# V in one transfer a pair instead of four, and GpSimd casting it across partition halves, later in its order

## The chip, the core and the metric

The kernel runs on one core of a Trainium2 chip. The core has five instruction streams that run side by side and meet through semaphores: PE (TensorE, matrix products), DVE (VectorE), ACT (ScalarE), POOL (GpSimd) and SP (SyncE, which only issues transfers). All transfers, whoever issues them, run on the core's 16 DMA engines. Two memories lie on the core: SBUF, with 128 partitions, and PSUM, where PE writes its products. The metric is the device time of one execution in microseconds (us). Three runs of the kernel before took 281.47, 281.88 and 282.79 us; the median is 281.88 us.

## The reference

An attention with a soft cap on the scores is followed by a soft mixture of experts whose tokens are the attention's outputs. The shapes are 8 batches, 12 heads, 448 tokens and 64 numbers a head, so 96 heads in all; then 3584 tokens of 768 numbers, 8 experts with 4 slots each, and a hidden width of 1024.

```python
scores = cap * tanh(q @ k.T / sqrt(64) / cap)          # cap = 30
attn   = softmax(scores)                               # over the keys
x      = (attn @ v)  -> (3584, 768)
logits = x @ phi                                       # (3584, 32)
d      = softmax(logits, over the tokens)
slots  = d.T @ x                                       # 32 slots
out_e  = relu(slots_e @ w1_e) @ w2_e                   # each expert, 4 slots
c      = softmax(logits, over the slots)
out    = c @ all the slots' outputs                    # (3584, 768), float32
```

Each token is a key and a value for the 448 tokens of its head. All inputs come as float32 from HBM.

## The kernel before, in words

**Pairs and quads.** Two heads make a pair (48 of them, numbered 0 to 47) and two pairs a quad (24). One pair's V is 2 x 448 x 64 float32 numbers, 224 KB. A head's 448 tokens are laid as 64 partitions of 7 tokens each: partition p of a half holds tokens 7p to 7p+6, and the 7 are called units here.

**The attention.** Q and K of a quad come by GpSimd's transfers, which also cast them to bf16 (`load`, line 290), are turned by PE (`transp`, L401, tiles `qps`, `kps`) and copied by DVE (`turned`, L410, L413). PE computes scores (`qk_chunk`, L444, tile `sc`, two buffers). ACT applies tanh to a chunk of them (`tanh_chunk`, L454) and the exponential to about two thirds of the chunks (`exp_part`, L458). For the other third DVE computes the exponential by a polynomial in eight steps (`poly_exp`, L478 to L486), with two scratch tiles, `xf` and `xp`. PE multiplies the result by V (`pv_mms`, L507), DVE normalises it (`norm_rec`, `norm_mul`, L515, L519), PE and DVE turn it (tile `xT`), and the logits and slot sums are gathered as it goes.

**V.** V of a pair lands in one of three buffers of `vraw` as float32, 128 partitions by 448 numbers. GpSimd casts it to bf16 into `vbd` (two buffers, one for each of two quads), which PE uses. In `vbd` each group of keys takes one unit from either head: the two heads' halves are arranged so that a matmul over 128 partitions sees both heads, with unit 3 of each head in a place of its own, whose other half is zero. For this the units of a head must lie partly in the upper partitions and partly in the lower. Before the change the transfers do that: `load_v` (L301 to L312) issues four of them, each 64 partitions by 4 or 3 units (1024 or 768 bytes a row). `vcast` (L417 to L423) is then one cast of 128 partitions by 6 units (L419) and two casts of 64 partitions by 1 unit (L423), all of which stay in their partitions.

**What sets the order.** Each engine runs its instructions in the order in which they were written. A string `PROGRAM` lists the steps, and `do` carries them out one by one: Q and T are scores and tanh, E an exponential on ACT, p a step of the polynomial, K and J the turning of K and Q, k and j its copies, A, t, B, u the four parts of a pair's product with V, r and m its normalisation, X, y, x the turning of the result, M one transfer of weights by GpSimd. At step u of pair n, `vcast_after(n)` writes the cast for pair n+4, which takes the place in `vbd` that pair n has just done with. A cast also issues the transfer of V three pairs on (SP). The steps K and J also issue the K and Q transfers two quads on, in GpSimd's order. So GpSimd's queue holds casts, K and Q transfers and weight transfers, each behind the one before.

**The weights.** GpSimd moves both weight matrices from HBM during the attention and casts them to bf16: w1 into SBUF (`w1b`), a part of w2 into SBUF (`w2u`), the rest back into HBM (`w2d`), 8 whole parts of 768 KB and 10 half parts of 384 KB. When the attention's buffers come free, SP reloads them (`reload`, L172 for whole and L174 for half parts, tiles `w2t`, two of them `raws`). The reloads are issued in one fixed order: half part 8, part 0, half parts 10 and 11, parts 1, 2, 3, half part 9, parts 4 to 7, half parts 12 to 17. Each waits for what lay at its place: half part 11 lies where `vraw` was, parts 1 and 2 take the places of `xf` and `xp`, half part 9 takes the place that the last two pairs' V had.

**The end.** After the last pair the two expert layers run (L882, L911), and the outputs go out by SP (L928) while DVE and ACT scale the tiles (L942, L944, L994, L996).

Of the kernel before, what the change touches and what calls it, by code (L numbers as in the profile page):

```python
# [18 lines left out]
P = 128  # L19
HP = 64  # L20
NT = 7
DH = 64
S = 448
CH = 6
CS = 3
# [5 lines left out]
W = DH + 1  # L31
# [7 lines left out]
def kernel(  # L39
# [224 lines left out]
    def part(x, off, *dims):  # L264
        return bass.AP(tensor=x.tensor, offset=x.offset + off, ap=[x.ap[0]] + [list(d) for d in dims])
# [8 lines left out]
    def quad_ap(nm, Q, h=None):  # L274
        b, hq = divmod(Q, NQB)
        off = (b * H + 4 * hq) * S * DH
        if h is not None:
            return bass.AP(tensor=srcs[nm].tensor, offset=off + 2 * h * S * DH,
                           ap=[[NT * DH, P], [1, NT * DH]])
        return bass.AP(tensor=srcs[nm].tensor, offset=off,  # L280
                       ap=[[NT * DH, P], [2 * S * DH, 2], [1, NT * DH]])
# [14 lines left out]
    def v_raw(Q, h):  # L296

        return raw_tile("kq"[h], (Q + 1) % 2).bitcast(F32) if Q == NQ - 1 else \
            vraw[:, (2 * Q + h) % NV, :]

    def load_v(Q, h):  # L301

        if Q < NQ:
            src = quad_ap("v", Q)
            long, short = slice(0, (CS + 1) * DH), slice((CS + 1) * DH, S)
            for r0, n, cols, at in ((0, 0, long, 0), (0, 1, short, CS + 1),
                                    (HP, 0, slice(0, CS * DH), CS + 1),
                                    (HP, 1, slice(CS * DH, S), 0)):
                sp.dma_start(out=v_raw(Q, h)[r0:r0 + HP, cols],
                             in_=bass.AP(tensor=src.tensor,  # L310
                                         offset=src.offset + (2 * h + n) * S * DH + at * DH,
                                         ap=[[NT * DH, HP], [1, cols.stop - cols.start]]))  # L312

    def init_vbd(n):
        t = vbds[n]
# [100 lines left out]

    def vcast(Q, h):  # L417
        raw, t = v_raw(Q, h), vbds[Q % 2]
        pool.tensor_copy(part(t[:, h, :, :], 0, [(CS + 2) * W, 2], [W, CS], [1, DH]),  # L419
                         part(raw, 0, [(CS + 1) * DH, 2], [DH, CS], [1, DH]))  # L420
        for n in range(2):
            r = slice(n * HP, n * HP + HP)
            pool.tensor_copy(t[r, h, CS + n, 0:DH], raw[r, CS * DH:(CS + 1) * DH])  # L423
        if 2 * Q + h + NV < NPAIR - 2:
            load_v(*divmod(2 * Q + h + NV, 2))

    def vcast_after(pr):

        Q, h = divmod(pr, 2)
        if Q + 2 < NQ:  # L430
            vcast(Q + 2, h)
# [252 lines left out]
    def spare(n, k=1):  # L684

        junk = home(k, [P, 4, P], F32, "junk")
        for _ in range(n):
            pe.matmul(junk, ones, wide(4), start=True, stop=True)

    def do(x, a, n):  # L690

        if x == "X":
            held["x", a] = home(n, [P, 2, S], BF16, "xps")
            x_mms(a, (0, 1, 2), held["x", a])
        elif x == "y":
            x_mms(a, (NF,), held["x", a])
        elif x == "t":
            pv_tail(a, 0, CA)
        elif x == "u":
            pv_tail(a, CA, NT)  # L700
            vcast_after(a)
        elif x == "x":
            x_copy(a, (0, 1) if a < NQ - 1 else (0,), held.pop(("x", a)))
        elif x == "e":
            es[a] = consts.tile([P, NG, NS], BF16, name="E", tag="E", bufs=3)
            act.activation(es[a], lps.pop(a), ACT.Exp)
        elif x == "R":
            held["R", a] = home(n, [P, 512], BF16, "eps")
            et_mms(a, held["R", a])
        elif x == "c":  # L710
            et_copy(a, held.pop(("R", a)))
        elif x == "W":
            held["W", a] = home(n, [P, NT], F32, "wps")
            ws_mms(a, held["W", a])
        elif x == "w":
            dve.reciprocal(winv[:, a, :], held.pop(("W", a)))
        elif x == "r":
            norm_rec(a, NT, pvs[a])
        elif x == "m":
            norm_mul(a, 0, NT, pvs.pop(a))  # L720
        elif x == "G":
            for i in range(a):
                pe.matmul(scores[n][:, i % CS, S:512], ones, ones[:, 0:512 - S], start=False,
                          stop=True, skip_group_check=True)
        elif x == "M":
            wjobs[a][0](*wjobs[a][1:])
        elif x == "O":
            reload_raw(a)
        elif x == "N":
            spare(a, n)  # L730
        elif x in "KJ":
            transp("kq"["KJ".index(x)], a, n)
        elif x in "kj":
            turned("kq"["kj".index(x)], a)
        else:
            {"Q": qk_chunk, "T": tanh_chunk, "E": exp_chunk, "p": poly_exp, "A": pv_first,
             "B": pv_rest, "L": logits, "S": slot_sums, "s": slot_add, "V": vcast,
             "F": fill}[x](*((a,) if n is None else (a, n)))
# [22 lines left out]

    for x, n in jobs:
        do(x, n[0], n[1] if len(n) > 1 else None)

    gl = NCH - 1
    last = NPAIR - 1
# [269 lines left out]
```

## Time and profile before

The profiled execution took 282.57 us on its own clock, of which the span, first to last instruction, is 280.7 us. All times below are counted from the start of that span.

| engine | busy, us | share of the span | instructions |
|---|---|---|---|
| ACT | 244.6 | 87% | 192 |
| DVE | 241.7 | 86% | 363 |
| PE | 234.1 | 83% | 4065 |
| POOL | 158.3 | 56% | 251 |

ACT and DVE are busy 9 tenths or more in every slice from about 14 us to about 225 us. That is the attention. After it come some 50 us in which no engine but the DMA is full. The page's line of DMA slices reads 9 (90% or more) nearly throughout. "Share of DMA" in a table of windows can exceed 1, since packets of two queues overlap on an engine.

In a timeline row the first number is the start, the second the time taken, then engine, line, operation, tiles written and read, shape, count, and in brackets how long the engine sat idle before and what released it. SPq means an issue in SP's queue.

### The profile page before, as it was taken

To read this page: it belongs to the slowest core of one execution; us is meant where nothing else is said; L and a number is where in the kernel's file an instruction comes from. 1 tells how busy PE (TensorE), PEld (TensorE's weight loads), DVE (VectorE), ACT (ScalarE), POOL (GpSimd) and SP (SyncE) were. 2 spreads that over 40 slices of the span, in tenths; PEclk is the share of its full clock that TensorE was granted. 3 is DMA by queue.
4 is the path that set the end of the run, shared out by engine and by line. 5 is a ranking of instruction groups with operands and counts; after the bars stand their busy time and mean duration, and the time that the engine had idled before them with its cause. 6 is when DMAs were issued, how large, how long until landed. Compare 5 with 4: busy or idle time off the path is not lost.

```text
span 280.7 us, 9632 instructions
## 1 busy us (share of the span) xinstructions
PE 234.1 (83%) x4065; PEld 149.4 (53%) x4065; DVE 241.7 (86%) x363; ACT 244.6 (87%) x192; POOL 158.3 (56%) x251
## 2 busy tenths in 40 slices
PE   8899879987898988888889989888889999798520
PEld 6435555564464756555656655655656675433200
DVE  3799999999999999999999999999999983258540
ACT  4999999999999999999999999999999992247420
POOL 8489567266877499858754969979342132000000
PEclk9999999999999999999999999999999999999955
DMA  6999999999999999999999999999999989989995
GB/s 177 224 168 221 222 222 206 222 212 221 224 231 191 216 214 227 222 228 224 226 225 226 222 229 224 217 223 218 219 229 243 277 329 403 398 308 366 407 413 243
DMA packets 51788, 69.56 MB, mean 248 GB/s; under 512 B 5921, under 2 KB 38305, under 8 KB 51745
## 3 DMA queue, kind: packets, MB, share of 16 engines
q0 software_dynamic: 27840, 35.77, 73.1%
q1 hardware_dynamic: 23616, 32.95, 35.9%
q8 instruction: 32, 0.52, 0.7%
q10 hardware_dynamic: 288, 0.23, 0.3%
q14 instruction: 12, 0.09, 0.1%
HBM read 93.68 MB, written 21.23 MB: 409 GB/s over the span
## 4 chain that ended last, share of the span: by engine, by line
ACT 68%; DVE 11%; DMA 9%; PE 5%; issue 2%; DVEq 0%; SPq 0%; ACTq 0%
ACT ex L454 30%; ACT ex L458 19%; ACT exg L454 9%; ACT exg L458 7%; DMA w2t<-w2d_None 4%; DMA out_dram<-ob 3%; PE so_ps L911 2%; DMA out_dram<-obh 1%; PE sc L444 1%; DMA raws<-in_q_dram 1%; DVE xp L484 1%; DVE xp L482 1%; DVE ex L485 1%; DVE xq L519 1%; DVE xp L481 1%
## 5 line engine op out<-in xcount | busy, mean ns | idle before, releaser
L454 ACT ACTIVATE ex<-sc 128x1344 f16<-128x1344 f32 (+1 forms) x87 | 108.9, 1372 | 1.3 <-PE sc L444 1.3
L444 PE MATMUL sc<-qT,kT 64*128 64x448 bf16 x384 | 67.8, 353 | 8.4 <-ACT ex L454 5.0
L458 ACT ACTIVATE ex<-ex 128x2688 bf16<-128x2688 f16 x27 | 68.4, 2546 | 0.0
L419 POOL CAST vbd<-vraw 128x384 bf16<-128x384 f32 x46 | 36.2, 787 | 43.1 <-DMA vraw<-in_v_dram 19.1
L507 PE MATMUL pv<-vbd,ex 128*128 128x65 bf16 (+2 forms) x1041 | 54.9, 200 | 5.7 <-DVE xT L576 1.4
L507 PEld LDWEIGHTS <-ex 128*128 128x128 bf16 (+1 forms) x1070 | 42.4, 101 | 21.1 <-issue 6.1
L423 POOL CAST vbd<-vraw 64x64 bf16<-64x64 f32 x92 | 51.9, 565 | 2.8
L454 ACT ACTIVATE exg<-sc 128x1344 f16<-128x1344 f32 x26 | 33.6, 1372 | 0.0
L444 PEld LDWEIGHTS <-kT 64*128 64x128 bf16 x384 | 18.7, 93 | 24.9 <-issue 11.4
L519 DVE TENSOR_TENSOR xq<-pv,rec 128x448 bf16<-128x448 f32 x47 | 28.5, 613 | 0.4
L458 ACT ACTIVATE exg<-exg 128x2688 bf16<-128x2688 f16 x11 | 27.7, 2520 | 0.0
L484 DVE TENSOR_TENSOR xp<-xp,xf 128x2688 f16<-128x2688 f16 x17 | 26.5, 1560 | 0.0
L482 DVE TENSOR_TENSOR xp<-xp,xf 128x2688 f16<-128x2688 f16 x17 | 26.4, 1556 | 0.0
L401 PEld LDWEIGHTS <-raws 128*64 128x64 bf16 x616 | 19.6, 109 | 11.2 <-issue 9.8
L290 POOL DMA_DIRECT2D raws<-in_q_dram x22 | 17.2, 782 | 11.9 <-PE qps L401 9.5
L485 DVE TENSOR_TENSOR ex<-ex,xp 128x2688 uint16<-128x2688 uint16 x15 | 23.1, 1539 | 0.0
L507 PE MATMUL pv<-vbd,exg 128*128 128x65 bf16 (+2 forms) x322 | 20.5, 199 | 2.9 <-DVE xq L519 1.9
L290 POOL DMA_DIRECT2D raws<-in_k_dram x22 | 17.0, 774 | 9.1 <-PE kps L401 5.0
L507 PEld LDWEIGHTS <-exg 128*128 128x128 bf16 (+1 forms) x322 | 14.3, 101 | 7.5 <-issue 4.1
L401 PE MATMUL kps<-ident,raws 128*64 128x128 bf16 x308 | 12.7, 221 | 3.4 <-DVE qT L413 0.9
L483 DVE TENSOR_SCALAR xp<-xp 128x2688 f16<-128x2688 f16 x17 | 15.0, 885 | 0.0
L481 DVE TENSOR_SCALAR xp<-xf 128x2688 f16<-128x2688 uint16 x17 | 14.7, 865 | 0.0
(138 smaller groups left out, 374.4 us busy)
## 6 DMA issues: line engine op xcount, KB each, us to landing
w1b<-in_moe_w_dram POOLq DMA_DIRECT2D x16, 768.0 KB, 10.2
w2d_None<-in_moe_w_dram POOLq DMA_DIRECT2D x8, 768.0 KB, 14.5
w2t<-w2d_None SPq DMA_DIRECT2D x8, 768.0 KB, 11.5
out_dram<-ob SPq DMA_DIRECT2D x8, 768.0 KB, 8.5
vraw<-in_v_dram SPq DMA_DIRECT2D x92, 64.0 KB, 5.9
raws<-in_q_dram POOLq DMA_DIRECT2D x22, 224.0 KB, 8.9
raws<-in_k_dram POOLq DMA_DIRECT2D x22, 224.0 KB, 8.8
vraw<-in_v_dram SPq DMA_DIRECT2D x92, 48.0 KB, 6.1
```

The lines of the kernel that those rows point to most:

```text
L290: pool.dma_start(out=t, in_=quad_ap(nm, Q))
L401: pe.transpose(dst, src[:, h, c * DH:(c + 1) * DH], ident)
L419: pool.tensor_copy(part(t[:, h, :, :], 0, [(CS + 2) * W, 2], [W, CS], [1, DH]), part(raw, 0, [(CS + 1) * DH, 2], [DH, CS], [1, DH]))
L423: pool.tensor_copy(t[r, h, CS + n, 0:DH], raw[r, CS * DH:(CS + 1) * DH])
L444: pe.matmul(sc[:, u, 0:S], qkT["k", Q][r, at:at + P], qkT["q", Q][r, :, n * HP:n * HP + HP], start=(c > 0 or n == 0), stop=(c > 0 or n == 1))
L454: act.activation(exs[j][:, half * CS + u0:half * CS + u1, :].bitcast(F16), sc[:, u0:u1, 0:S], ACT.Tanh, scale=qk_scale / cap)
L458: act.activation(exs[j][:, u0:u1, :], exs[j][:, u0:u1, :].bitcast(F16), ACT.Exp, scale=cap)
L482: lambda: dve.tensor_tensor(p, p, f, op=ALU.mult),
L484: lambda: dve.tensor_tensor(p, p, f, op=ALU.mult),
L485: lambda: dve.tensor_tensor(y, y, p, op=ALU.add),
L507: pe.matmul(out_, exs[j][:, u, q0:q0 + (HP if tail else P)], v_, start=(c == 0 and g == gs[0] < NF), stop=(c >= NT - 2), skip_group_check= ...
L519: dve.tensor_tensor(xq[Q][:, h, s0:s1, :], pv[:, 0:s1 - s0, 0:DH], recs.pop(pr).to_broadcast([P, s1 - s0, DH]), op=ALU.mult)
```

## The change

V of a pair is loaded by one transfer of 128 partitions by 7 units, 1792 bytes a row: the first head in the lower 64 partitions, the second in the upper. The casts now bring the units to their partition half: for each head one cast of 4 units within its half and one of 3 units into the other half, four casts of 64 partitions in place of three. The cast for pair n+4 is no longer written at step u of pair n but at the next step m of any pair, so that steps written between u and that m (K, J and M among them) come ahead of it in GpSimd's order. The order on PE, DVE and ACT stays as it was.

```diff
     def load_v(Q, h):
         if Q < NQ:
-            src = quad_ap("v", Q)
-            long, short = slice(0, (CS + 1) * DH), slice((CS + 1) * DH, S)
-            for r0, n, cols, at in ((0, 0, long, 0), (0, 1, short, CS + 1),
-                                    (HP, 0, slice(0, CS * DH), CS + 1),
-                                    (HP, 1, slice(CS * DH, S), 0)):
-                sp.dma_start(out=v_raw(Q, h)[r0:r0 + HP, cols],
-                             in_=bass.AP(tensor=src.tensor,
-                                         offset=src.offset + (2 * h + n) * S * DH + at * DH,
-                                         ap=[[NT * DH, HP], [1, cols.stop - cols.start]]))
+            sp.dma_start(out=v_raw(Q, h), in_=quad_ap("v", Q, h))
...
     def vcast(Q, h):
         raw, t = v_raw(Q, h), vbds[Q % 2]
-        pool.tensor_copy(part(t[:, h, :, :], 0, [(CS + 2) * W, 2], [W, CS], [1, DH]),
-                         part(raw, 0, [(CS + 1) * DH, 2], [DH, CS], [1, DH]))
-        for n in range(2):
-            r = slice(n * HP, n * HP + HP)
-            pool.tensor_copy(t[r, h, CS + n, 0:DH], raw[r, CS * DH:(CS + 1) * DH])
+        lo, hi = slice(0, HP), slice(HP, P)
+        for own, other, own0, other0 in ((lo, hi, 0, 0), (hi, lo, CS + 1, CS + 2)):
+            rows = raw[own].rearrange("p (c d) -> p c d", d=DH)
+            pool.tensor_copy(t[own, h, own0:own0 + CS + 1, 0:DH], rows[:, 0:CS + 1, :])
+            pool.tensor_copy(t[other, h, other0:other0 + CS, 0:DH], rows[:, CS + 1:NT, :])
...
+    due = []
+
     def do(x, a, n):
...
         elif x == "u":
             pv_tail(a, CA, NT)
-            vcast_after(a)
+            due.append(a)
...
     for x, n in jobs:
         do(x, n[0], n[1] if len(n) > 1 else None)
+        while due and x in "m":
+            vcast_after(due.pop(0))
```

## The prediction

> **What bounds the kernel now.** I read the page's first and fourth parts, then busy times by window, then the waits, then the timelines of the end.
>
> ```profile
> span 280.7 us, 9632 instructions
> PE 234.1 (83%) x4065; PEld 149.4 (53%) x4065; DVE 241.7 (86%) x363; ACT 244.6 (87%) x192; POOL 158.3 (56%) x251
> ...
> ACT 68%; DVE 11%; DMA 9%; PE 5%; issue 2%; DVEq 0%; SPq 0%; ACTq 0%
> ```
>
> Windows: time, then busy time of PE, PEld, DVE, ACT, POOL, then clock, share of DMA, GB/s.
>
> ```profile
> 8.00:232.00 224.00, 198.02 (x3572) 129.70 (x3570) 219.03 (x322) 223.72 (x160) 149.68 (x223) 1.00 1.15 225
> 168.00:210.00 42.00, 37.00 (x693) 24.77 (x692) 41.33 (x59) 42.00 (x31) 31.25 (x49) 1.00 1.25 221
> 224.00:226.00 2.00, 2.00 (x38) 1.40 (x37) 2.00 (x5) 2.00 (x2) 1.88 (x5) 1.00 0.64 234
> 232.00:234.00 2.00, 1.81 (x24) 0.95 (x22) 1.15 (x4) 0.82 (x3) 0.00 (x0) 1.00 1.01 390
> 248.00:250.00 2.00, 2.00 (x29) 0.58 (x22) 1.48 (x3) 1.42 (x3) 0.00 (x0) 1.00 0.53 193
> 250.00:252.00 2.00, 1.91 (x28) 0.66 (x26) 1.09 (x2) 0.90 (x3) 0.00 (x0) 1.00 0.85 303
> ```
>
> From 8 to 232 us ACT is busy 223.72 of 224 us. It can't gain there; it can only be made to wait. DVE has 5.0 us to spare in the same stretch, GpSimd 74.3. After 232 the reloads of the weights and the output's transfers decide, with one wait between.
>
> ```profile
> PE so_ps L911 <- DMA w2t<-w2d_None: 1.6, 1, 1.6
> ```
>
> ```profile
> 214.53 0.32 PE L507 MATMUL pv<-vbd,ex 128*64 128x65 bf16 x8
> ...
> 245.20 0.35 PE L911 MATMUL so_ps<-w2t,hpad 128*32 128x384 bf16 x4 [1.59 <-DMA w2t<-w2d_None]
> ...
> 250.29 1.03 PE L911 MATMUL so_ps<-w2t,hpad 128*32 128x384 bf16 x20
> ```
>
> PE stands still for 1.59 us until whole part 7 has landed. Why it lands so late is read from SP's queue and GpSimd's.
>
> ```profile
> 207.96 4.43 SPq L309 DMA_DIRECT2D vraw<-in_v_dram  x4
> ...
> 215.83 0.33 SPq L174 DMA_DIRECT2D w2t<-w2d  x1
> ...
> 224.86 0.32 SPq L174 DMA_DIRECT2D w2t<-w2d  x1
> ```
>
> ```profile
> 205.17 0.53 POOL L423 CAST vbd<-vraw 64x64 bf16<-64x64 f32 x2
> ...
> 223.65 0.71 POOL L419 CAST vbd<-vraw 128x384 bf16<-128x384 f32 x1 [9.26 <-DMA vraw<-in_v_dram]
> ```
>
> V of pair 45 is issued in four pieces from 207.96 to 212.39, though its buffer was free with the cast that ended at 205.70, and its last piece lands just before 223.65. PE had been done with the place in `vbd` since 214.85 (row at 214.53). So GpSimd idles 9.26 us, the cast of pair 45 ends near 224.84, and only then can SP issue the reload of half part 11 (224.86), which lies where `vraw` was. Every later reload stands behind it. In the window 224 to 226 the DMA engines are 0.64 busy, at 234 GB/s, where 232 to 234 shows 390.
>
> **The change, part by part.**
>
> *One transfer instead of four.* The next fence: time from issue to landing of V's transfers, then of the K and Q transfers.
>
> ```profile
> DMA to landing us min/median/max: 2.4/6.0/11.6
> ...
> DMA to landing us min/median/max: 3.8/8.9/13.8
> ```
>
> Four issues took 4.43 us here; one takes about 1.1 us of SP. Pairs 46 and 47, just ahead of pair 45, likewise take 2 issues, not 8. Pair 45's transfer can then leave when its buffer is free: 205.70, plus 1.0 us for a longer cast (below), 206.7. It lands 2.4 to 11.6 us later, by 209.1 to 218.3. PE's 214.85 is then the later condition or nearly so; with a cast of at most 2.9 us half part 11 goes out between 217.8 and 221.2, not at 224.86. Next in SP's queue is part 1, which takes the place of `xf`.
>
> ```profile
> 97.99 1.56 DVE L482 TENSOR_TENSOR xp<-xp,xf 128x2688 f16<-128x2688 f16 x1
> ...
> 220.85 1.55 DVE L484 TENSOR_TENSOR xp<-xp,xf 128x2688 f16<-128x2688 f16 x1
> ```
>
> DVE reads `xf` last in L484, until 222.40. So the stream of reloads starts at 222.4 instead of 224.86, 2.5 us sooner, with half part 11 already out of its way. PE needs 1.59 of it. From 245.20 to 251.3 PE's rows are back to back, so no more than 1.59 us can be had: PE itself is late next. Bounds 0 (the stream starts no sooner) and -1.59; I take **-1.6 us**, as 2.5 covers it.
>
> The output follows PE. In 248 to 252 the DMA engines were idle for 0.47 x 2 + 0.15 x 2 = 1.24 us, partly because the last reloads still ran beside the first outputs. Bounds 0 and -1.2; I take **-0.3**, near the end where what PE has ready decides.
>
> At the head, V of pair 1 comes some 4 us sooner, but pair 0's first product comes long after its cast and ACT has no gap: 0.
>
> *Four casts instead of three.* First GpSimd alone, in a stretch where nothing held it up, then one beside DVE's row at 97.99, then the whole groups.
>
> ```profile
> 12.37 0.51 POOL L419 CAST vbd<-vraw 128x384 bf16<-128x384 f32 x1 [3.66 <-DMA vraw<-in_v_dram]
> 12.82 0.23 POOL L423 CAST vbd<-vraw 64x64 bf16<-64x64 f32 x1
> 13.11 0.23 POOL L423 CAST vbd<-vraw 64x64 bf16<-64x64 f32 x1
> ...
> 98.09 1.56 POOL L423 CAST vbd<-vraw 64x64 bf16<-64x64 f32 x1
> ```
>
> ```profile
> L419 POOL CAST vbd<-vraw 128x384 bf16<-128x384 f32 x46 | 36.2, 787 | 43.1 <-DMA vraw<-in_v_dram 19.1
> ...
> L423 POOL CAST vbd<-vraw 64x64 bf16<-64x64 f32 x92 | 51.9, 565 | 2.8
> ```
>
> 384 numbers took 0.51 us, 64 took 0.23: 0.875 ns a number on 0.174 us. A cast of 4 units (256) is then 0.40, of 3 units (192) 0.34, four casts 1.48 against 0.97 (13.34 less 12.37). A cast that meets one of DVE's operations from SBUF to SBUF waits for its end: the one at 98.09 ended at 99.65, DVE's at 99.55. So the mean pair took (36.2 + 51.9) / 46 = 1.92 us, 1.98 times the free one. With the same factor the new pair takes 2.93 us: **+1.0 us a pair** on GpSimd. That a cast crosses to the other half is in no row; I price it as a cast of its width, 0.34, at least, and 1.56 (the row at 98.09) at most, which would add another 2.4 us a pair. I take the first, since the row of the same kind and width class is nearest.
>
> On these durations the Trainium skill, GPSIMD Engine Reference, section 2.1 (Instruction dispatch), would say better: each of GpSimd's cores serves 16 partitions and starts the next instruction when its own share is done, so casts on different halves could overlap. The rows at 12.82 and 13.11, one on either half, do not overlap (0.29 us apart, 0.23 long); by the rule the four casts would come to some 0.8 us a pair, by the rows 1.48, and the rows decide.
>
> What covers the +1.0: pair 45 apart, casts end well ahead of their product. The narrowest in the middle is pair 31.
>
> ```profile
> 156.81 1.16 POOL L423 CAST vbd<-vraw 64x64 bf16<-64x64 f32 x2
> ```
>
> ```profile
> 162.85 0.35 PE L507 MATMUL pv<-vbd,ex 128*128 128x130 bf16 x3
> ...
> 179.58 0.58 PE L401 MATMUL kps<-ident,raws 128*64 128x128 bf16 x14 [0.83 <-DVE xq L519]
> ```
>
> It is done at 157.97 and needed at 162.85, 4.9 us. If GpSimd lags by more, PE waits, and behind it the scores that ACT needs.
>
> *Later in GpSimd's order.* The cast no longer holds back the K and Q transfers, but three or four casts may now stand in a row ahead of one. Tightest is K of quad 20.
>
> ```profile
> 169.77 0.74 POOL L290 DMA_DIRECT2D raws<-in_k_dram  x1
> ```
>
> Issued at 169.77 and landing in a median 8.9 us, it is there at 178.7; PE turns it at 179.58. The new order takes one cast from ahead of Q's transfer of this quad (before: cast 34, K, cast 35, Q; now cast 34, K, Q, cast 35), none from ahead of K's, and the casts of pairs 32 to 34 before both are 1.0 us longer each, less what GpSimd's idle time swallows. One or two such places may lose a microsecond each; the two score buffers hide about half. 0 to +1.8; I take **+0.4**.
>
> *What DVE pays.* A waiting cast enters when DVE's operation ends and can hold up the next one.
>
> ```profile
> L484 DVE TENSOR_TENSOR xp<-xp,xf 128x2688 f16<-128x2688 f16 x17 | 26.5, 1560 | 0.0
> L485 DVE TENSOR_TENSOR ex<-ex,xp 128x2688 uint16<-128x2688 uint16 x15 | 23.1, 1539 | 0.0
> ...
> L483 DVE TENSOR_SCALAR xp<-xp 128x2688 f16<-128x2688 f16 x17 | 15.0, 885 | 0.0
> ```
>
> ```profile
> L483 DVE TENSOR_SCALAR xp<-xp x17: 810/856/1107, 15.1 to 219.2; 128x2688 f16<-128x2688 f16 x17
> ...
> L484 DVE TENSOR_TENSOR xp<-xp,xf x17: 1508/1543/1752, 16.4 to 220.9; 128x2688 f16<-128x2688 f16 x17
> ...
> L485 DVE TENSOR_TENSOR ex<-ex,xp x15: 1500/1545/1558, 18.4 to 222.4; 128x2688 uint16<-128x2688 uint16 x15
> ```
>
> Means above medians: 29 x 17 + 17 x 17 - 6 x 15 ns = 0.69 us in three of the polynomial's eight steps, so about 1.8 us in all are lost to GpSimd now. The numbers cast per pair rise from 384 + 64 + 64 = 512 to 896, 1.75 times, so +1.4 us. DVE has 5.0 us to spare but spread thin, ACT 0.28: between 0 and +1.4 reach the end; I take **+0.7**.
>
> **The sum.** -1.6 - 0.3 + 0.4 + 0.7 = -0.8 us on the profiled execution's 282.57: 281.8. That execution lies 0.69 us above the median of 281.88, so against the median **281.1 us**, within 0.5% (1.4 us, about what a measurement can tell from no change).
>
> **The rivals.**
>
> *Nothing is lost in the attention.* ACT stays full, DVE's 1.4 us vanish in its 5.0 us to spare, and the end gives 1.6 + 0.3 to 1.2: 279.1 to 280.0. For it: every cast but the last three had 4.9 us or more. Against it: ACT has nothing to spare, so any late product shows.
>
> *GpSimd becomes the bound; slower.* In 168 to 210 it is busy 31.25 of 42 us and casts 9 pairs (35 to 43): 10.75 idle, 1.19 us a pair. My +1.0 leaves it full at 40.3. Above +1.19 it falls behind, from about 112 us on for 21 pairs: at +1.4 by 4.4 us, near pair 31's 4.9 and beyond the K transfers' 0.9. Its lag then delays ACT. With crossing casts at 1.56 us it would be far behind. I put it at 283.4 to 287. For it: 1.19 against 1.0 is little. Against it: the 1.98 was taken where casts met a full DVE.
>
> *DVE becomes the bound; slower.* The casts' numbers take 48 x 512 x 0.875 ns = 21.5 us now, of which DVE loses 1.8, one part in twelve; after, 48 x 896 x 0.875 ns = 37.6 us. If three parts in ten of that came to stand in DVE's way, 11.3 us, that is 9.5 more than now, 4.5 beyond the 5.0 to spare, less 1.9 at the end +2.6: 284.5. It decides from a little over a quarter on. For it: casts now queue up and enter between every two operations of DVE. Against it: the one in twelve of now. The Trainium skill, Advanced Engine Details and Errata, section VectorE Performance Modes (Mode Summary), says that GpSimd and VectorE operations in two-port modes block each other; the waits of casts agree (1.56 us at 98.09), the blocking of DVE is small so far.
>
> *The change does not do what it says at the end.* Pair 45's V still lands late, say because weights crowd it; then +0.4 + 0.7 stay: 283.0.
>
> **How the numbers follow.** Forecast 0.38 (own range 280.5 to 282.6); nothing lost 0.27; GpSimd the bound 0.20; DVE the bound 0.10; no gain at the end 0.05. Faster by over 0.5% (below 280.47) is the first rival, 0.27; slower (above 283.29) the next two, 0.30; the rest 0.43. The range runs from 279.6, leaving out the best tenth, to 285.0, leaving out the worst of the GpSimd case.
>
> **What would show it.** Half part 11's reload at 218 to 221 and part 1's at 222.4; no wait of PE in L911; GpSimd 9.26 us idle gone; some 2.9 us of casts a pair (2.4 would favour the first rival, over 3.1 the second); GpSimd near 95% in 168 to 210; DVE's L483 and L484 means up by some 20 ns. I am wrong if ACT shows idle time of over 1 us between 8 and 232, or if crossing casts take much over 0.34 us with nothing beside them.

## The result, and the profile after

The changed kernel takes 289.5 us (median of four runs, 288.85 to 290.42) where the kernel before, run beside it, takes 282.24 (281.47 to 282.79). The ratio is 1.026, with a 95% interval of 1.022 to 1.030: it is slower by 7.3 us, and 4.5 us above the upper end of the predicted range. The profiled execution took 288.85 us, with a span of 287.1, 6.4 us more than the span before.

First the page's head, its part 1 and the engines' shares of the chain that ended last.

```profile
span 287.1 us, 9428 instructions
...
PE 237.6 (83%) x4065; PEld 151.0 (53%) x4065; DVE 246.3 (86%) x363; ACT 245.9 (86%) x192; POOL 209.2 (73%) x299
...
DVE 49%; POOL 18%; DMA 15%; PE 10%; issue 3%; ACT 2%; DVEq 0%; POOLq 0%; SPq 0%; ACTq 0%
```

The chain has changed its owner: ACT had 68% of it and now has 2%, DVE has 49% and GpSimd, which had none, 18%. GpSimd is busy 50.9 us longer, DVE 4.6.

The windows (time, busy time of PE, PEld, DVE, ACT, POOL, clock, share of DMA, GB/s), the casts' groups, and three of DVE's polynomial steps.

```profile
8.00:232.00 224.00, 195.23 (x3454) 126.01 (x3453) 220.25 (x311) 221.31 (x157) 197.21 (x262) 0.99 1.11 213
168.00:210.00 42.00, 37.02 (x678) 23.96 (x676) 41.56 (x62) 41.94 (x31) 39.90 (x51) 1.00 1.16 208
```

```profile
L414 POOL CAST vbd<-vraw 64x256 bf16<-64x256 f32 x92 | 77.7, 844 | 15.7 <-DMA vraw<-in_v_dram 7.1
...
L415 POOL CAST vbd<-vraw 64x192 bf16<-64x192 f32 x92 | 59.2, 643 | 5.5
...
L476 DVE TENSOR_TENSOR xp<-xp,xf 128x2688 f16<-128x2688 f16 x17 | 27.1, 1596 | 0.0
...
L477 DVE TENSOR_TENSOR ex<-ex,xp 128x2688 uint16<-128x2688 uint16 x15 | 23.6, 1574 | 0.0
...
L475 DVE TENSOR_SCALAR xp<-xp 128x2688 f16<-128x2688 f16 x17 | 15.4, 906 | 0.0
```

The four casts of a pair take (77.7 + 59.2) / 46 = 2.98 us, and in 168 to 210 GpSimd is busy 39.90 of 42 us. DVE's three steps have risen from 1560, 1539 and 885 ns to 1596, 1574 and 906.

Where the 6.4 us of span lie is read at the end of the attention: ACT's last exponential and its first copy behind it, before and after.

```profile
229.60 2.63 ACT L771 ACTIVATE ex<-ex 128x1536 bf16<-128x1536 f16 x3
232.82 0.37 ACT L822 COPY xT<-xpl 128x256 bf16<-128x256 bf16 x1 [0.59 <-PE xpl L562]
```

```profile
233.30 2.63 ACT L767 ACTIVATE ex<-ex 128x1536 bf16<-128x1536 f16 x3
239.78 0.37 ACT L818 COPY xT<-xpl 128x256 bf16<-128x256 bf16 x1 [3.86 <-PE xpl L554]
```

Three terms add up to it. The attention ends 3.7 us later (235.93 against 232.23). ACT then waits 3.86 us for the last pair's result, not 0.59, which is 3.3. From there to the end of the span it takes 47.3 us instead of 47.9, a gain of 0.6. What ACT waits for at 239.78 is found in SP's queue and GpSimd's.

```profile
197.09 19.45 SPq L304 DMA_DIRECT2D vraw<-in_v_dram  x5
216.72 0.80 SPq L304 DMA_DIRECT2D raws<-in_v_dram  x2
218.45 0.33 SPq L304 DMA_DIRECT2D vraw<-in_v_dram  x1
...
219.91 12.89 SPq L174 DMA_DIRECT2D w2t<-w2d  x2
```

```profile
224.03 0.39 POOL L414 CAST vbd<-vraw 64x256 bf16<-64x256 f32 x1 [2.32 <-DMA vraw<-in_v_dram]
...
230.79 0.40 POOL L414 CAST vbd<-vraw 64x256 bf16<-64x256 f32 x1 [2.67 <-DMA vraw<-in_v_dram]
...
235.57 0.35 POOL L415 CAST vbd<-raws 64x192 bf16<-64x192 f32 x1
```

Pair 45's V goes out at 218.45, since the cast that frees its buffer ends there, and lands just before 230.79. The casts of pairs 45, 46 and 47 then follow one another until 235.92. Half part 11, whose reload had left at 224.86, leaves at 232.49 (the second of the two at 219.91), and PE still waits on a whole part for 1.3 us. How far GpSimd is behind by then shows in its own queue. Here are the timeline's rows of its issue of the last quad's K, before and after.

```profile
191.75 0.73 POOL L290 DMA_DIRECT2D raws<-in_k_dram  x1
```

```profile
204.62 0.92 POOL L290 DMA_DIRECT2D raws<-in_k_dram  x1
```

The issue comes 12.9 us later, while ACT is only 3.7 us behind at the end of the attention. In the middle the lag costs the attention next to nothing: ACT's tanh that starts at 99.46 before starts 3.1 us later, the one at 181.97 3.4 us later, while the K transfers of quads 17 to 20 between them go out 5 to 10 us later.

One thing more stands in the windows, the granted TensorE clock (third number from the end), for two stretches of the changed kernel:

```profile
62.00:65.40 3.40, 3.37 (x33) 1.99 (x33) 3.40 (x4) 2.40 (x2) 3.22 (x4) 0.50 1.11 236
232.65:236.06 3.41, 3.34 (x57) 3.05 (x55) 1.14 (x4) 3.25 (x4) 2.85 (x8) 0.50 0.83 281
```

PE ran at half clock there, where the kernel before has full clock until 267 us. Each stretch begins while PE waits or just after: PE stands still for 1.41 us until 62.03 (for DVE) and for 1.79 us until 232.10 (for the casts of pair 45). Not every such wait brings it; the kernel before waits 1.34 us at the first place and keeps its full clock. The loss as a whole does not need it either: the run of 289.25 us had a mean granted clock of 0.975, the profiled run of the kernel before 0.976.

### The profile page after: what moved, and what is told of

Read it like the earlier page. It is cut to its first block, busy times and chain, and to the rows that moved or that the text cites. A ratio compares the mean times of both kernels' runs of the same rounds, so it can differ in the third digit from the quotient of the medians.

```text
span 287.1 us, 9428 instructions
## 1 busy us (share of the span) xinstructions
PE 237.6 (83%) x4065; PEld 151.0 (53%) x4065; DVE 246.3 (86%) x363; ACT 245.9 (86%) x192; POOL 209.2 (73%) x299
## 4 chain that ended last, share of the span: by engine, by line
DVE 49%; POOL 18%; DMA 15%; PE 10%; issue 3%; ACT 2%; DVEq 0%; POOLq 0%; SPq 0%; ACTq 0%
POOL vbd L414 7%; DMA vraw<-in_v_dram 7%; DVE ex L477 6%; DVE xp L476 5%; DVE xp L474 5%; POOL vbd L415 5%; DVE xq L511 5%; DMA w2t<-w2d_None 4%; DVE ex L470 4%; DVE xp L473 3%; DVE xf L472 3%; DVE ex L478 3%; DVE kT L402 3%; DVE xp L475 3%; DVE qT L405 3%
## 5 line engine op out<-in xcount | busy, mean ns | idle before, releaser
L446 ACT ACTIVATE ex<-sc 128x1344 f16<-128x1344 f32 (+1 forms) x87 | 107.4, 1315 | 3.4 <-PE sc L436 2.3
L414 POOL CAST vbd<-vraw 64x256 bf16<-64x256 f32 x92 | 77.7, 844 | 15.7 <-DMA vraw<-in_v_dram 7.1
L436 PE MATMUL sc<-qT,kT 64*128 64x448 bf16 x384 | 68.6, 357 | 6.5 <-ACT ex L446 2.9
L450 ACT ACTIVATE ex<-ex 128x2688 bf16<-128x2688 f16 x27 | 67.0, 2490 | 0.0
L499 PE MATMUL pv<-vbd,ex 128*128 128x65 bf16 (+2 forms) x1041 | 56.3, 203 | 9.8 <-POOL vbd L414 2.1
L415 POOL CAST vbd<-vraw 64x192 bf16<-64x192 f32 x92 | 59.2, 643 | 5.5
L499 PEld LDWEIGHTS <-ex 128*128 128x128 bf16 (+1 forms) x1070 | 43.8, 103 | 25.2 <-issue 7.3
L436 PEld LDWEIGHTS <-kT 64*128 64x128 bf16 x384 | 18.0, 94 | 23.9 <-issue 10.5
L450 ACT ACTIVATE exg<-exg 128x2688 bf16<-128x2688 f16 x11 | 27.1, 2467 | 0.0
L476 DVE TENSOR_TENSOR xp<-xp,xf 128x2688 f16<-128x2688 f16 x17 | 27.1, 1596 | 0.0
L474 DVE TENSOR_TENSOR xp<-xp,xf 128x2688 f16<-128x2688 f16 x17 | 27.0, 1591 | 0.0
L477 DVE TENSOR_TENSOR ex<-ex,xp 128x2688 uint16<-128x2688 uint16 x15 | 23.6, 1574 | 0.0
```

Of the source, the lines that this page charges most:

```text
L414: pool.tensor_copy(t[own, h, own0:own0 + CS + 1, 0:DH], rows[:, 0:CS + 1, :])
L415: pool.tensor_copy(t[other, h, other0:other0 + CS, 0:DH], rows[:, CS + 1:NT, :])
L436: pe.matmul(sc[:, u, 0:S], qkT["k", Q][r, at:at + P], qkT["q", Q][r, :, n * HP:n * HP + HP], start=(c > 0 or n == 0), stop=(c > 0 or n == 1))
L446: act.activation(exs[j][:, half * CS + u0:half * CS + u1, :].bitcast(F16), sc[:, u0:u1, 0:S], ACT.Tanh, scale=qk_scale / cap)
L450: act.activation(exs[j][:, u0:u1, :], exs[j][:, u0:u1, :].bitcast(F16), ACT.Exp, scale=cap)
L474: lambda: dve.tensor_tensor(p, p, f, op=ALU.mult),
```

## The experiments

### The three parts, one at a time

`order_only` is the kernel before with the later place in GpSimd's order and nothing else.

```diff
         elif x == "u":
             pv_tail(a, CA, NT)
-            vcast_after(a)
+            due.append(a)
...
         do(x, n[0], n[1] if len(n) > 1 else None)
+        while due and x in "m":
+            vcast_after(due.pop(0))
```

> The kernel before with only the later order of the casts; four transfers and three casts a pair stay. If the longer casts are the cause (GpSimd falls behind), this is within 1 us of the kernel before (282.2 us), GpSimd's casts still 1.9 us a pair, and GpSimd busy about 31 of 42 us in 168 to 210. If the later order is the cause, it carries most of the 7.3 us: 287 or more.

Measured: ratio 1.003, interval 1.000 to 1.007. The later place alone costs a third of a per cent or nothing.

`casts_only` is the changed kernel with the casts back at their old place.

```diff
         elif x == "u":
             pv_tail(a, CA, NT)
-            due.append(a)
+            vcast_after(a)
```

> The changed kernel with the casts in their old place, at step u. If the longer casts are the cause, it is as slow as the changed kernel (289.5 us) or slower by up to 3 us, since K and Q transfers now stand behind casts of 3.0 us. If the later order is the cause, it comes back to within 2 us of 282.2.

Measured: ratio 1.015 (1.010 to 1.020). The one transfer and the four casts make the kernel slower at the old place too. The later place adds some 1.1% to that, against 0.3% alone; the intervals are too wide to say that the parts do not simply add.

`four_in_place` keeps the four transfers and the old order, so nothing crosses, but makes four casts of 4, 3, 4 and 3 units of them.

```diff
-        pool.tensor_copy(part(t[:, h, :, :], 0, [(CS + 2) * W, 2], [W, CS], [1, DH]),
-                         part(raw, 0, [(CS + 1) * DH, 2], [DH, CS], [1, DH]))
-        for n in range(2):
-            r = slice(n * HP, n * HP + HP)
-            pool.tensor_copy(t[r, h, CS + n, 0:DH], raw[r, CS * DH:(CS + 1) * DH])
+        for own, at in ((slice(0, HP), ((0, 0, CS + 1), (CS + 1, CS + 2, CS))),
+                        (slice(HP, P), ((CS, CS + 1, CS + 1), (0, 0, CS)))):
+            rows = raw[own].rearrange("p (c d) -> p c d", d=DH)
+            for c0, u0, n in at:
+                pool.tensor_copy(t[own, h, u0:u0 + n, 0:DH], rows[:, c0:c0 + n, :])
```

> The kernel before, with its four transfers and its order, but with each pair cast by four instructions of 64 partitions (256, 192, 256, 192 numbers), none crossing to the other half. If GpSimd's time is the cause, this alone costs as much as the change: 288 to 292 us, casts near 3.0 us a pair. If crossing the halves or the single transfer is the cause, it stays within 2 us of 282.2.

Measured: ratio 1.030 (1.021 to 1.039), span 290.2. This is as slow as the whole change, or slower, without a cast that crosses and without the one transfer. So the four casts alone bring a loss of this size. A cast that stays in its half is not cheaper than one that crosses:

```profile
L423 POOL CAST vbd<-vraw x184: 339/402/1823, 7.7 to 234.8; 64x256 bf16<-64x256 f32 x92, 64x192 bf16<-64x192 f32 x92
```

```profile
L414 POOL CAST vbd<-vraw x92: 391/900/1682, 7.7 to 231.7; 64x256 bf16<-64x256 f32 x92
L415 POOL CAST vbd<-vraw x92: 342/347/1652, 8.2 to 232.1; 64x192 bf16<-64x192 f32 x92
```

The first fence is this kernel, the second the changed one (ns: least, median, most); the least of 3 units is 339 ns in place and 342 crossing. `casts_only`, which differs by the transfers and by where the 3 units go, is at 1.015. The 1.5% between them is not simply the price of four transfers. Until 158 us the attention of `four_in_place` is 1.7 us late, that of `casts_only` 2.8; what sets them apart is a late K near 174 and the half clock behind it, shown under `until_36`. The transfers may have a share in that, since K and Q land in a median of 8.1 us in `casts_only` and 9.0 in `four_in_place`. The Trainium skill, DMA: Bandwidth & Descriptors, section Rules for kernel authors, advises one transfer over all 128 partitions in place of two to disjoint halves. The two ratios lie on its side, but no run here shows the share of the transfers by itself.

`no_crossing` is the changed kernel with both crossing casts left out from pair 4 on, so that 6 of 14 units of V keep old values.

```diff
-            pool.tensor_copy(t[other, h, other0:other0 + CS, 0:DH], rows[:, CS + 1:NT, :])
+            if 2 * Q + h < 4:
+                pool.tensor_copy(t[other, h, other0:other0 + CS, 0:DH], rows[:, CS + 1:NT, :])
```

> The changed kernel with the two crossing casts left out from pair 4 on, so that 3 of 7 units of V keep the numbers of an earlier pair; the time is that of less work on GpSimd. If GpSimd's time is the cause, the loss goes (two casts, some 1.9 us a pair as before) and the gain that was foretold for the end shows: 279 to 282 us, pair 45's cast no later than 219. If the single transfer or the later order is the cause, it stays at 286 or more.

Measured: ratio 1.002 (0.998 to 1.005). Without the crossing casts the loss is gone. What the end should have gained is not there, or something takes it; the later place is still in this kernel.

`no_crossing_early` is the same kernel with the casts at their old place.

> The changed kernel with both crossing casts left out from pair 4 on (6 of 14 parts of V are not cast there, left out of the computation) and the casts at their old place in GpSimd's order. It is what the one transfer alone is worth with a GpSimd that has time to spare. With the later place the same work gave 1.002. Theory 1 (the later place costs about what it costs the kernel before, 0.3%, and the transfer gains 0.6 us at the end): 0.996 to 1.000. Theory 2 (the one transfer gains 1.5%, as between the two runs with four casts, 1.015 and 1.030): 0.985 to 0.990. Theory 3 (neither is worth anything here): 1.000 to 1.004.

Measured: ratio 0.998 (0.995 to 1.000), span 280.8, GpSimd busy 132.9 us. Theory 1 fits. So one transfer for all pairs, with GpSimd's work made light, is worth about a quarter of a per cent, by the interval half a per cent at most. Its trace shows why it is so little: the part behind the attention is 1.3 us shorter than before, but the attention ends 1.4 us later (233.60), and DVE is busy 1.5 us longer.

### How much GpSimd's load costs, and through which engine

`one_crossing` leaves out one of the two crossing casts from pair 4 on (3 of 14 units of V keep old values).

```diff
-            pool.tensor_copy(t[other, h, other0:other0 + CS, 0:DH], rows[:, CS + 1:NT, :])
+            if 2 * Q + h < 4 or own is lo:
+                pool.tensor_copy(t[other, h, other0:other0 + CS, 0:DH], rows[:, CS + 1:NT, :])
```

> The changed kernel with one of its two crossing casts left out from pair 4 on, so that 3 of 14 parts of V are not cast there (left out of the computation). It stands half way between the changed kernel (two crossing casts, ratio 1.026) and the one with none (1.002), by casts of 0.34 us free, or 0.64 us as the rows with VectorE's share have it. Theory 1 (a threshold: GpSimd falls behind only when it is nearly full, and 2.98 - 0.64 = 2.34 us a pair leaves it some 20% idle): ratio 1.000 to 1.006, no idle ScalarE over 1 us at the end. Theory 2 (every cast costs its share, by lengthening VectorE's operations): ratio 1.011 to 1.017.

Measured: ratio 1.006 (1.004 to 1.008), at the upper edge of the threshold theory and well below half of 2.6%. Its page (head, part 1, chain), the window of the attention, ACT's row behind the last exponential, and GpSimd's issue of the last K:

```profile
span 282.8 us, 9384 instructions
...
PE 235.3 (83%) x4065; PEld 150.0 (53%) x4065; DVE 245.9 (87%) x363; ACT 245.8 (87%) x192; POOL 182.0 (64%) x255
...
DVE 67%; PE 17%; ACT 6%; DMA 4%; issue 2%; SPq 0%; DVEq 0%; ACTq 0%
```

```profile
8.00:235.00 227.00, 199.04 (x3570) 129.78 (x3568) 223.20 (x320) 225.12 (x160) 173.39 (x227) 1.00 1.12 225
```

```profile
236.03 0.37 ACT L819 COPY xT<-xpl 128x256 bf16<-128x256 bf16 x1 [0.62 <-PE xpl L555]
```

```profile
195.09 1.24 POOL L290 DMA_DIRECT2D raws<-in_k_dram  x1
```

GpSimd has 54 us to spare in these 227. The last K goes out at 195.09, 3.3 us after the kernel before's, in step with an attention that ends 3.2 us later (235.41). In the middle K of quads 17 and 18 goes out 7.7 and 6.1 us later, but by quad 19 that is down to 1.0. No load is late at the end. Even so the attention is 3.2 us longer, and the chain is DVE's by two thirds: DVE is busy 245.9 us, 4.2 more than before, nearly as much as in the changed kernel. So there are two losses. One comes by way of DVE and is there with a GpSimd that keeps up. The other, the difference between 282.8 and 287.1 (by the ratios 2.0%, 5.6 us), comes when GpSimd falls behind.

`dve_plus` measures the first by itself: the kernel before, in which DVE takes every second pair's reciprocal twice.

```diff
-        dve.reciprocal(recs[pr], pv[:, 0:n, DH:W])
+        for _ in range(1 + (pr % 2 == 0)):
+            dve.reciprocal(recs[pr], pv[:, 0:n, DH:W])
```

> The kernel before with one edit: VectorE takes the reciprocal of every even pair's row sums twice, 24 more instructions of 0.197 us, 4.7 us of VectorE's time, and nothing more for GpSimd. In the changed kernel VectorE was busy 4.6 us longer (246.3 against 241.7) and the attention ended 3.7 us later; with one crossing cast less it was busy 4.2 us longer and the attention ended 3.2 us later, although GpSimd had time to spare. Theory 1 (VectorE sets the attention's pace, so its time counts nearly in full, whatever lengthens it): the attention ends 3 to 4.5 us later, ratio 1.010 to 1.016. Theory 2 (VectorE has slack; late V and late K/Q are what delays the attention): under 1 us later, ratio 1.000 to 1.004.

Measured: ratio 1.008 (1.004 to 1.012), between the two theories.

```profile
PE 236.1 (83%) x4065; PEld 149.1 (52%) x4065; DVE 246.0 (86%) x387; ACT 246.1 (86%) x192; POOL 149.3 (52%) x251
...
DVE 56%; PE 18%; ACT 15%; DMA 4%; issue 2%; POOL 1%; DVEq 0%; ACTq 0%; POOLq 0%
```

With 4.3 us more of DVE's time, and GpSimd no busier than before, the attention of this execution ends 3.5 us later (235.69), and the chain turns from ACT's to DVE's just as it did after the change. Over the runs 4.3 us of DVE cost 0.76% of 282 us, 2.1 us (1.0 to 3.3 by the interval), about half; the profiled execution is the slowest of the ten. The 4.6 us that the change adds to DVE's time are therefore worth some 2 us, by the runs, and up to 3.5 by this one trace. The traces agree among themselves: DVE's extra time and the later end of the attention are 1.5 and 1.4 us in `no_crossing_early`, 4.2 and 3.2 in `one_crossing`, 4.3 and 3.5 here, 4.6 and 3.7 in the changed kernel.

### The end

`early_last` is the changed kernel, in which SP issues V of pairs 46 and 47 ahead of pair 44's.

```diff
         if 2 * Q + h + NV < NPAIR - 2:
-            load_v(*divmod(2 * Q + h + NV, 2))
+            held_v.append(divmod(2 * Q + h + NV, 2))
+            if 2 * Q + h + NV != NPAIR - 4:
+                load_v(*held_v.pop())
...
             turned("kq"["kj".index(x)], a)
+            if x == "j" and a == NQ - 2:
+                load_v(*held_v.pop())
```

> The changed kernel with one edit: SyncE issues the V loads of the last two pairs (46, 47) ahead of that of pair 44, not behind it. In the changed kernel ScalarE stood idle 3.86 us from 235.93 to 239.78, against 0.59 us before; pair 45's V was issued at 218.45 and landed at 230.64, behind pairs 46's and 47's, which were issued at 216.72 and 217.15. Theory 1 (two losses: V that lands late at the end, 3.3 us, and an attention that ends 3.7 us later): pairs 46 and 47 are issued by about 207, pair 45's V lands before 226, the idle stretch falls under 1 us, and the ratio to the kernel before falls from 1.026 to about 1.012 to 1.016. Theory 2 (GpSimd is simply out of time, the order of the loads does not matter): its last cast ends as late as in the changed kernel and the ratio stays at 1.023 to 1.030.

Measured: ratio 1.020 (1.016 to 1.024), between the two theories. PE's and ACT's waits near the end:

```profile
PE so_ps L912 <- DMA w2t<-w2d_None: 2.9, 2, 1.6
...
ACT xT L823 <- PE xpl L557: 1.2, 1, 1.2
```

ACT's wait for the last pair fell from 3.9 us to 1.2, so it did hang on the order of the loads. Yet 1.6 us of that came back in PE's wait for the reloads, 2.9 us against 1.3, because half part 11's reload still stands behind the late casts (230.17). SP was held up by pair 43's load, which waited until 210.49 for a cast, so pairs 46 and 47 went out at 211, not at 207.

`until_36` gives GpSimd the last twelve pairs to catch up: the changed kernel to pair 35, then the old transfers and casts, with the later place throughout.

```diff
+    ONE = 36
...
-        if Q < NQ:
+        if Q < NQ and 2 * Q + h < ONE:
+            sp.dma_start(out=v_raw(Q, h), in_=quad_ap("v", Q, h))
+        elif Q < NQ:
```

> The changed kernel up to pair 35, with the later place in GpSimd's order throughout; the last twelve pairs are loaded by four transfers and cast by three instructions as before. GpSimd has these twelve pairs to catch up, so that V does not land late at the end. Theory 1 (the loss has two parts, an attention that VectorE's longer operations delay by 2 to 3.5 us over 46 pairs, and 3.3 us at the end where V lands late): 36/46 of the first stays, 1.6 to 2.7 us, the second goes and so does the 0.6 to 1.1 us gained in the tail; no idle ScalarE over 1.2 us between the last attention step and the next: ratio 1.006 to 1.012. Rival (the loss is GpSimd's lag alone, and it is made good once GpSimd catches up): 0.999 to 1.004. Rival (the loss follows the number of long casts wherever they stand): 36/46 of 2.6%, ratio 1.018 to 1.024.

Measured: ratio 1.018 (1.011 to 1.024). I had expected 1.006 to 1.012. The idle time behind the last exponential did go (0.64 us), but these waits of PE are new or longer, and ACT's timeline shows what the second of them costs:

```profile
PE so_ps L925 <- DMA w2t<-w2d_None: 2.0, 2, 1.6
...
PE qps L404 <- DMA raws<-in_q_dram: 1.8, 1, 1.8
```

```profile
216.04 1.29 ACT L464 ACTIVATE ex<-sc 128x1344 f16<-128x1344 f32 x1 [2.10 <-PE sc L454]
```

GpSimd had issued the last Q late, and the scores behind it cost ACT 2.1 us at 216.04. The two other heavily loaded kernels show the same kind of wait, on K near 174: `casts_only` in the first fence, `four_in_place` in the second.

```profile
PE kps L393 <- DMA raws<-in_k_dram: 1.5, 1, 1.5
```

```profile
PE kps L401 <- DMA raws<-in_k_dram: 2.6, 1, 2.6
```

Such a wait costs more than its own length, as the window from 174 to 188 shows in the kernel before, `casts_only` and `four_in_place`, in this order:

```profile
174.00:188.00 14.00, 12.20 (x240) 8.41 (x241) 13.78 (x20) 14.00 (x11) 12.08 (x18) 1.00 1.27 220
```

```profile
174.00:188.00 14.00, 11.84 (x231) 8.46 (x232) 11.20 (x17) 11.65 (x10) 11.32 (x17) 0.88 1.23 222
```

```profile
174.00:188.00 14.00, 12.56 (x170) 8.52 (x172) 8.30 (x13) 8.85 (x7) 7.74 (x14) 0.52 1.23 216
```

ACT (the fourth busy time) does 14.00, 11.65 and 8.85 us of work in these 14. The granted clock is at half for 3.4 us from 175.64 in `casts_only` and for 13.65 us from 174.50 in `four_in_place`. `until_36` has 3.4 us of half clock from 212.52, behind its wait for Q. So a late load costs ACT first PE's wait and then products at half clock. How much of each ACT loses was not tried by itself.

The lag is paid once or twice in each of these kernels, where the queue happens to be late: K at 174, Q at 210, V at 231, the reloads near 250. Taking away one such place moved it to another. The ratio of `until_36` alone would also suit a loss that goes by the number of long casts (1.018 to 1.024); `one_crossing`, at 1.006 instead of 1.013, speaks against that as the whole rule. How the lag grows with the number of pairs is not settled by these runs.

### The change at the end alone

`one_from_44` is the kernel before up to pair 43; only pairs 44 to 47 have the one transfer and the four casts, at the old place.

```diff
+    ONE = 44
...
-        if Q < NQ:
+        if Q < NQ and 2 * Q + h >= ONE:
+            sp.dma_start(out=v_raw(Q, h), in_=quad_ap("v", Q, h))
+        elif Q < NQ:
```

> The kernel before with its own order and its own loads and casts up to pair 43; pairs 44 to 47 alone have the change's one transfer and four casts. GpSimd's load before that is the kernel before's. Prediction: the wait on the whole part 7 near the end (1.6 us of TensorE) goes and the output ends 0.3 us sooner: ratio 0.993 to 0.995. Rival (what the changed kernel's trace shows from the last attention step to the end: 47.3 us against 47.9): 0.6 us, ratio 0.998. Rival (the casts of the last four pairs stand in one line in front of the last products): 1.5 us later, ratio 1.005.

Measured: ratio 0.996 (0.994 to 0.998), median 281.91 us beside 283.12 for the kernel before: 0.4% or about 1.1 us faster than the kernel before, and the fastest of all that were run, beside `one_from_46`. Span 279.8. First SP's queue, then PE's row.

```profile
215.50 3.68 SPq L174 DMA_DIRECT2D w2t<-w2d  x2
222.67 3.28 SPq L172 DMA_DIRECT2D w2t<-w2d_None  x3
```

```profile
245.38 0.34 PE L950 MATMUL op<-so,ET 128*128 128x384 bf16 x1
246.71 0.32 PE L950 MATMUL op<-so,ET 128*128 128x384 bf16 x1 [0.98 <-issue]
```

Half part 11's reload leaves at 218.86 (the end of the two issues at 215.50), part 1's at 222.67, and PE has no wait in L921. But between the first two products of the output there is now a gap of 0.98 us, which the profile puts down to nothing ("issue"). Before, these two followed each other within 0.50 us. So of the 1.59 us some 0.6 is left at this place.

`one_from_46` and `one_from_36` move the border.

> The kernel before up to pair 45; pairs 46 and 47 alone, whose V goes to the buffers that K and Q leave, have the change's one transfer and four casts. With pairs 44 to 47 the ratio was 0.996 and the wait of 1.6 us on the whole part 7 was gone. Theory 1 (the gain is that SyncE comes past the V loads to the reloads sooner, and the eight quarters of pairs 46 and 47 were what held it): ratio 0.995 to 0.997, no such wait. Theory 2 (the four quarters of pair 45, issued one behind another as the buffers and queues come free, still hold it): 0.999 to 1.001 and the wait stays.

> The kernel before up to pair 35; pairs 36 to 47 have the change's one transfer and four casts, at the old place in GpSimd's order. With pairs 44 to 47 alone the ratio was 0.996. Theory 1 (each pair with four casts costs VectorE about 4.6 / 46 = 0.1 us, 0.8 us for eight more pairs, and GpSimd's lag is not yet there): ratio 0.998 to 1.000. Theory 2 (the loss comes when GpSimd falls behind, and twelve pairs in a row at 2.98 us a pair are enough for that, as V then comes late at the end): ratio 1.005 to 1.012.

From pair 46 on: 0.996 (0.992 to 1.000), no wait on a whole part, theory 1. From pair 36 on: 1.004 (1.000 to 1.008), between the theories. In `one_from_36` the attention ends only 0.3 us later than before (232.56), as DVE's account had it, but half part 11's reload waits for the casts until 225.55, and PE waits:

```profile
PE so_ps L921 <- DMA w2t<-w2d_None: 2.2, 2, 1.6
```

Its last K goes out 4.2 us later than before (195.99). Twelve pairs in a row are enough for a lag that eats the gain, eight more than in `one_from_44`.

## Why the prediction was wrong

**The terms that failed.** In the profiles the sum missed by 7.2 us, -0.8 foretold against +6.4. The end was put at -1.9 and came at +2.7 (3.3 of ACT's wait less 0.6), DVE at +0.7 where the attention ends 3.7 later, K and Q at +0.4 where no long wait for them shows. Behind the first of these is GpSimd's load, behind the second what casts do to DVE.

**GpSimd's price was right as a mean.** A free crossing cast of 3 units takes 0.34 us, as priced, and a pair takes 2.98 us against 2.93.

**What that load does was wrong, and this is the step that failed.** The prediction let GpSimd fall behind only above +1.19 us a pair, the idle time of 168 to 210 over its 9 pairs, and set against it +1.0, a mean over the whole run. In that window itself the casts, before and after, are these:

```profile
L419 POOL CAST vbd<-vraw 128x384 bf16<-128x384 f32 x10 | 10.1, 1006 | 9.4 <-issue 6.4 <-PE wps L636 2.4 <-PE pv L507 0.2
L423 POOL CAST vbd<-vraw 64x64 bf16<-64x64 f32 x20 | 8.4, 420 | 0.6
```

```profile
L414 POOL CAST vbd<-vraw 64x256 bf16<-64x256 f32 x18 | 15.2, 845 | 1.1 <-DMA vraw<-in_v_dram 0.2
L415 POOL CAST vbd<-vraw 64x192 bf16<-64x192 f32 x17 | 12.4, 730 | 1.0
```

A pair there took 1006 + 2 x 420 ns = 1.85 us before and takes 2 x (845 + 730) ns = 3.15 us now: +1.30, above the prediction's own +1.19. By its own sum that is 31.25 + 9 x 1.30 = 43.0 us in a window of 42. GpSimd waits for only 0.2 us in it; the other 1.9 us of its idle time are gaps of under 0.1 us between instructions. So 39.90 us is a full queue, and its nearness to the 40.3 foretold is luck: GpSimd gets less done in it than before, 35 casts at four a pair (under 9 pairs) against 30 at three (10 pairs), and 16 issues against 19. Its K transfers slip from 6.2 us late (quad 20) to 12.9 (quad 23). Pair 31's 4.9 us were not where it was paid; at the end the casts of pairs 45 to 47 stood right before the last products. Of the rival "GpSimd becomes the bound", the mechanism happened, and with more cost: the end of its range was 287. `one_crossing`, whose casts take 2 x 780 + 654 ns = 2.21 us a pair, has its last K in step with ACT. Where between 2.21 and 2.98 us a pair the lag sets in was not tried.

**DVE's term was too small.** The prediction had +1.4 us of DVE's time, of which 0.7 reach the end; the trace has +4.6, of which about 2 count by `dve_plus`. In the changed kernel's trace I counted, for each of the 51 tensor-tensor steps of the polynomial, the casts that ran within it: the mean is 1537 ns with none (7 steps), 1563 with one (18), 1620 with two (26). That is 18 x 26 + 26 x 83 ns = 2.6 us above the undisturbed 1537; the same count in the trace before (20 with none at 1543 ns, 18 with one at 1543, 13 with two at 1576) gives 0.4 us. What tells is whether a cast is already running when the step starts: the 33 such steps take 1616 ns on the mean, the 11 into which a cast comes only later 1540. All of DVE's growth lies in the polynomial's eight steps, by the rows of the two traces 1.9 us in these three and 3.4 in the other five; DVE's other work took 0.7 less. The numbers cast per pair, by which the prediction had scaled, do not set it: `one_crossing` casts 704 a pair and adds 4.2 us, `no_crossing_early` casts 512 as before and adds 1.5. The Trainium skill, SBUF — State Buffer, section Who interferes with whom, says that GpSimd and a VectorE operation with two inputs from SBUF hold a shared port pair as an exclusive lock, so that the one that starts first blocks the other. The trace agrees in kind, both ways: casts wait for DVE's end (0.34 us free, up to 1.65), and L476 takes up to 1784 ns instead of 1540. The row at 98.09, which the prediction sets beside the two-port modes, waits behind such an operation with two inputs (L482) and bears on this rule instead. The rival "DVE becomes the bound" put the time at 284.5, 2.6 us above the kernel before; `one_crossing` is 0.6%, 1.7 us, above the one run beside it, so its closeness in microseconds (284.46) is in part luck. The two rivals were priced as alternatives and came together.

**The gain at the end was right in its chain and wrong in its premise.** With a GpSimd that keeps up, half part 11 leaves at 218.86 (foretold 217.8 to 221.2), part 1 at 222.67 (222.4), and PE's wait goes. In the changed kernel half part 11 left at 232.49, 7.6 us later than before, since the foretold 206.7 for pair 45's V rested on a cast only 1.0 us later; it was issued at 218.45. And "PE itself is late next" let all of PE's wait count: 0.98 of the 1.59 us turn up again a few instructions on. Together with the output, the end is worth 1.1 us by the runs of `one_from_44`, not 1.9.

**K and Q late, +0.4.** In the changed kernel no wait on K or Q is among its longer ones, though they were issued up to 12.9 us later; in three variants one such wait took 1.5, 1.8 and 2.6 us. Such a wait, where it came, was longer than the microsecond foretold, and the reason was not one cast more ahead of Q: GpSimd's whole queue was late.

**The account now.** Some 2 to 3.5 us by way of DVE, 4.3 us by GpSimd's lag (287.1 less 282.8, of it 3.3 in ACT's wait for the last pair), less about 1 us at the end: 5.3 to 6.8, of 6.4 in the profiles and 7.3 in the medians. The lag's part is taken as a difference of two kernels and was not measured by itself; by the ratios it is 5.6 us. The half clock is part of it and was not taken apart.

The prediction named its own refutation: ACT idle for over 1 us between 8 and 232. In the changed kernel ACT is idle 2.7 us in all from 8 to 235.93, the longest 1.0, against 0.28 before. Of these, 1.00 and 0.45 us (until 64.80 and 66.54) fall in or just behind the half clock from 62. The signs that did come, 2.98 us a pair and 95% in 168 to 210, could not tell the forecast from its rival, since both have a full GpSimd.

## What to carry to other kernels

When work is added to an engine that issues loads, frees buffers and works in one queue, price it in the stretch where the engine is fullest, and not by the mean of the run (here +1.30 us a pair against +1.0). Then look at how late its own loads go out (here 12.9 us), and leave it time to spare (at 76% busy its last load was in step here). Where two engines are both nearly full, price a third one's work by what it adds to their operations, not only by its own time. And apply a change where its gain lies: in the last four pairs it won 0.4%, in all 48 it lost 2.6%.

## What the runs showed of the hardware that I had not expected

A GpSimd cast from one half of the partitions to the other costs no more than one that stays: 342 against 339 ns for 64 x 192. In these traces a cast lengthens a two-input operation of DVE when it is already running as the operation starts: 1616 ns against 1539 for the rest in the changed kernel's trace; a cast that comes later waits for the operation's end, and that one takes 1540. A wait of PE of 1.4 to 2.6 us can be followed by half clock, in the traces above 3.4 us of it in four places and 13.65 us in one, while 1.34 and 1.59 us in the kernel before were not. And the 0.98 us gap in PE between two products of the output, for which the profile names no releaser, is there with 0.98 us in `one_from_44`, `one_crossing` and `no_crossing_early` and with 0.67 us in `one_from_46`, all kernels in which PE no longer waits for the whole part; in `dve_plus`, where it does not wait for it either, there is no such gap. Its cause is open.
